# A transformer block's forward and backward pass: bulk transfers behind transposed rows, a later kv^T block, and gate-gradient chunks one block ahead

## The chip, the cores and the metric

The kernel runs on one core of a Trainium2 chip. The metric is the device time of one execution in microseconds (us), and less is better. The core has five engines that work side by side, each through its own instructions in order: TensorE (PE, with its weight loads shown as PEld), VectorE (DVE), ScalarE (ACT), GpSimd (POOL) and SyncE (SP), which in this kernel only issues transfers (DMAs). Engines wait for each other by semaphores.

## The reference

One transformer block with pre-layernorms, linear attention and a gated MLP, its output and its gradients. B = 1, S = 2048 rows, D = 640, H = 32 heads of 20, F = 1728, all in bf16. In short:

```python
def A(x, wqkv, wo):                       # linear attention
    q, k, v = split_heads(x @ wqkv)
    phi = lambda t: where(t > 0, t + 1, exp(t)) + 1e-6
    pq, pk = phi(q), phi(k)
    kv = einsum("bhsd,bhse->bhde", pk, v)
    z  = einsum("bhsd->bhd", pk)
    den = einsum("bhqd,bhd->bhq", pq, z)[..., None] + 1e-6
    return merge_heads(einsum("bhqd,bhde->bhqe", pq, kv) / den) @ wo

def B(x, w1, w3, w2):                     # gated MLP
    return (silu(x @ w1) * (x @ w3)) @ w2

h  = x + A(layernorm(x), wqkv, wo)
h2 = h + B(layernorm(h), w1, w3, w2)      # output 0
# outputs 1 to 6: gradients of sum(h2 * grad_out) for x, wqkv, wo, w1, w3, w2
```

## The kernel before

The rows are worked on in 16 tiles of 128 (t = 0 to 15) and in four chunks of 512 rows (c = 0 to 3). The order of the instructions on every engine is the order in which the program is written; only the memory pools and their semaphores are filled in by the framework. The stages around the change are these.

**Stage 1, the loop over t in range(ST).** For each tile, `p1_mm(t, D)` makes k from the transposed normalized rows `pqT`, and `phi` evicts it with two ACT activations (L294, L295) and two DVE operations that are held back (`held`) and run later (L298, L299). `v_steps[t]` lists what DVE does in step t: "S" is the statistics of a tile (`stat`), "N" its normalization on DVE (`p1_norm`), R one held-back piece. "A", "B" and "L" are normalizations after `phi`: "A" ahead of `q_tile`, "B" and "L" behind it. Even tiles above 8 are normalized on ACT (L165), the others on DVE (L160). For tiles from 8 on `p1_norm` also issues, on SP, the transposing DMA of that tile's rows into `pqT` (L250); the matmuls of `p1_mm(t)` wait for it. The big transfers go through the same queue: `trickle` says after which tile a piece of w1, w3 or wqkv is loaded, and `outs` after which tile the normalized rows (`xn_out`) and phi(k) (`group_out`) are stored. Each x load, `load_x(a, b)`, brings tiles a to b - 1.

**Stage 2, after that loop.** `m_part(m, tiles)` accumulates block m of the product of phi(k) and the normalized rows; `m_end` evicts it and transposes it into `mT`; `kvT_block(m, acc)` multiplies it with the v weights (L448) and writes its masked diagonal blocks to `bd` with one DVE multiply (L211). Between them `q_tile(t)` makes q of a tile, and `r_row(t)` makes the denominators on DVE (L373 to L380). The accumulators of `kvT_block` and `q_tile` alternate between the two buffers of the PSUM tag "big". Then `ps.release()` ends that PSUM pool and the pool "pap" takes the same banks. Its first steps are `q_late(10, f2_mT)`, where `f2_mT` (L717, tile `trm`, tag "at") transposes the last block of m between the two halves of q of tile 10.

**Stage 3, the MLP loop.** Block n = c * FT + fc, with FT = 14. `mlp(c, fc, ...)` first calls `mlp_ghh`, which makes a chunk of the gate gradient's input, `ghh` (five matmuls of 512 columns and an ACT eviction, L419), for a later block; `ghh` tiles hold two chunks and have four buffers. Then come gate and up (L394), ACT's four evictions, part of the second product of the chunk before (`o2_steps`), and side steps: `f2_at` (attention output of the next chunk's tiles, L654), `f2_hn` (their second layernorm, with a store of the rows) and `f2_ht` (the transposing DMA of these rows). `drain` runs one of seven DVE operations per pair of blocks (L829) at a time. `r_steps[c][fc]` lists further steps: `r_den` and `r_end` (denominators of tiles 8 to 15, using PSUM tag "at", which `f2_at` uses too) and loads.

The rest, the backward products, is not touched by the change.

## Time and profile before

| | us |
|---|---|
| three timed runs | 822.13, 822.12, 821.39 (median 822.12) |
| the profiled execution | 820.91 |
| its span in the profile | 819.1 |
| PE busy in the span | 814.1 |
| DVE busy | 452.4 |
| ACT busy | 323.6 |
| GpSimd busy | 130.9 |

Every value comes from one program on one core. The times are of runs without a profile, and the span is that of one execution with it, 1.8 us shorter than that execution's own time. TensorE's granted clock is full in all but the first moments. Instruction rows in the profile give the start in us from the span's start, the duration, the engine, the source line, the operation and the tile written <- tiles read.

### The profile page before, as it was taken

How to read it: one execution, taken by the hardware profiler on the slowest of the kernel's cores; microseconds unless marked ns; L12 is line 12 of the kernel's file. 1: busy time of each engine (PE TensorE's matmuls, PEld its weight loads, DVE VectorE, ACT ScalarE, POOL GpSimd, SP SyncE). 2: the span in 40 equal slices, each digit the busy share in tenths (PEclk: the TensorE clock that was granted, in tenths of full speed). 3: DMA queues.
4: the chain of work that ended last, by engine and by line, in shares of the span. 5: the costliest groups of instructions: out<-in, count | busy, mean ns of one | idle time of the engine just before them, and what ended most of it. 6: DMA issues, size and time to landing. Idle time of an engine off the chain costs nothing.

```text
span 819.1 us, 13944 instructions
## 1 busy us (share of the span) xinstructions
PE 814.1 (99%) x5420; PEld 512.8 (63%) x5420; DVE 452.4 (55%) x973; ACT 323.6 (40%) x603; POOL 130.9 (16%) x193
## 2 busy tenths in 40 slices
PE   9999999999999999999999999999999999999998
PEld 6677544555555555777777777777777777544444
DVE  7859987998898566300057777772781544200000
ACT  7856688665565666011122212222212334211111
POOL 2233333333222212100001111110220000000000
PEclk9999999999999999999999999999999999999999
DMA  9899699796485556999977877259974997967751
GB/s 264 219 290 239 166 244 327 225 245 173 127 211 156 169 170 167 222 261 226 257 176 180 211 197 200 58 107 187 287 195 93 181 194 159 239 164 186 160 141 36
DMA packets 323873, 157.88 MB, mean 193 GB/s; under 512 B 242784, under 2 KB 317056, under 8 KB 323808
## 3 DMA queue, kind: packets, MB, share of 16 engines
q1 hardware_dynamic: 281040, 116.18, 61.6%
q0 software_dynamic: 7328, 24.48, 8.7%
q10 hardware_dynamic: 35440, 16.34, 7.7%
q8 instruction: 42, 0.69, 0.4%
q14 instruction: 23, 0.19, 0.1%
HBM read 47.09 MB, written 51.13 MB: 120 GB/s over the span
## 4 chain that ended last, share of the span: by engine, by line
PE 96%; DVE 2%; ACT 1%; issue 0%; DMA 0%; POOL 0%; ACTq 0%; DVEq 0%
PE mm L394 20%; PE job L1346 20%; PE ghn L1142 14%; PE gxn L1515 8%; PE gw L1097 7%; PE o L910 4%; PE o L856 3%; PE gwo L1230 3%; PE big L267 3%; PE gr L1199 3%; PE dkv L1452 3%; PE macc L429 2%; PE at L654 2%; PE mm L267 1%; PE dkv L1380 1%; DVE st L147 1%
## 5 line engine op out<-in xcount | busy, mean ns | idle before, releaser
L1346 PE MATMUL job<-gb,hnN 128*128 128x496 bf16 (+3 forms) x576 | 116.8, 366 | 0.0
L1142 PEld LDWEIGHTS <-ggb 128*128 128x128 bf16 x864 | 84.5, 98 | 32.8
L1346 PEld LDWEIGHTS <-hnN 128*128 128x128 bf16 x576 | 55.8, 98 | 61.0
L394 PE MATMUL mm<-pqT,w 128*128 128x512 bf16 x405 | 93.8, 379 | 0.1
L394 PEld LDWEIGHTS <-w 128*128 128x128 bf16 x540 | 52.5, 98 | 63.4 <-issue 1.4
L1350 ACT CAST obs<-job 128x496 bf16<-128x496 f32 (+4 forms) x56 | 28.5, 510 | 123.7 <-PE job L1346 120.9
L1142 PE MATMUL ghn<-w13a,ggb 128*128 128x320 bf16 x448 | 63.5, 299 | 0.0
L1157 DVE SCALAR_TENSOR_TENSOR wb<-gs,hnb 128x640 f32<-128x640 bf16 x16 | 13.2, 825 | 88.7 <-ACT gs L1154 88.7
L1142 PE MATMUL ghn<-w13b,ggb 128*128 128x320 bf16 x416 | 61.4, 299 | 0.0
L394 PE MATMUL mm<-g2T,w2T 128*128 128x512 bf16 x240 | 59.6, 379 | 0.0
L1097 PE MATMUL gw<-g,hb 128*128 128x320 bf16 x416 | 56.8, 299 | 0.0
L1207 POOL TENSOR_TENSOR sz<-Zb,g_h 128x640 f32<-128x640 bf16 x16 | 20.2, 1261 | 197.7 <-DVE g_h L1208 197.7
L1097 PEld LDWEIGHTS <-hb 128*128 128x128 bf16 x416 | 40.6, 98 | 16.0 <-issue 0.3
L419 ACT CAST ghh<-mm 128x512 bf16<-128x512 f32 x48 | 28.3, 589 | 47.7 <-PE mm L394 40.1
L793 ACT ACTIVATE sig<-mm 128x512 bf16<-128x512 f32 x56 | 33.9, 605 | 26.4 <-PE mm L394 21.1
L1154 ACT ACTIVATE gs<-ghn 128x640 bf16<-128x640 f32 x16 | 11.3, 704 | 78.8 <-PE ghn L1142 73.9
L394 PEld LDWEIGHTS <-w2T 128*128 128x128 bf16 x260 | 25.4, 98 | 23.4
L267 PEld LDWEIGHTS <-pqT 128*128 128x128 bf16 x320 | 30.7, 98 | 13.7 <-ACT pqT L259 1.5
L267 PE MATMUL big<-wqkv,pqT 128*128 128x320 bf16 x250 | 38.6, 299 | 0.6 <-ACT pqT L259 0.3
L1346 PEld LDWEIGHTS <-g 128*128 128x128 bf16 x320 | 31.0, 98 | 11.5
L829 DVE TENSOR_TENSOR gate<-gate,sig 128x1024 bf16<-128x1024 bf16 x28 | 19.3, 689 | 33.2 <-ACT gate L804 30.5
L910 PE MATMUL o<-w,hhT 128*128 128x320 bf16 x224 | 35.0, 299 | 0.0
(219 smaller groups left out, 1369.9 us busy)
## 6 DMA issues: line engine op xcount, KB each, us to landing
hh_d<-hhT SPq DMA_DIRECT2D x24, 256.0 KB, 2.7
gg_d<-gate POOLq DMA_DIRECT2D x24, 256.0 KB, 4.3
gg_d<-ghh POOLq DMA_DIRECT2D x24, 256.0 KB, 3.4
ggb<-gg_d SPq DMA_DIRECT2D x6, 896.0 KB, 5.4
ggb<-gg_d ACTq DMA_DIRECT2D x6, 832.0 KB, 5.7
ggb<-gg_d SPq DMA_DIRECT2D x2, 1728.0 KB, 12.7
x_sb<-in_A_x_dram SPq DMA_DIRECT2D x5, 640.0 KB, 5.9
pk_d<-pk_all SPq DMA_DIRECT2D x4, 640.0 KB, 6.6
```

The source lines that it names most:

```text
L267: T.matmul(acc, lhsT=pqT[:, c, t * P:(t + 1) * P], rhs=wqkv[:, c, n0:n0 + HD], start=(c == 0), stop=(c == DT - 1))
L394: T.matmul(acc[:], lhsT=w[:, c, fc * P:(fc + 1) * P], rhs=rhs[:, c, :], start=(c == 0), stop=(c == DT - 1))
L419: A.copy(out=ghh[n // 2][:, n % 2, :], in_=acc[:])
L793: A.activation(sig[:, i, :], gp[:], AF.Sigmoid)
L856: T.matmul(accs[i, j][:, 0:HD], lhsT=hhT[c][:, fc, i * P:(i + 1) * P], rhs=w2[:, fc, j * HD:(j + 1) * HD], start=(first and fc == 0), stop ...
L910: T.matmul(o2["ps"][:, 0:HD], lhsT=hhT[c][:, fc, i * P:(i + 1) * P], rhs=w2[:, fc, j * HD:(j + 1) * HD], start=(fc == 0), stop=(fc == FT - 1))
L1097: T.matmul(acc[:, j, 0:HD], lhsT=hb[b][:, t, i * P:(i + 1) * P], rhs=g2[:, t, j * HD:(j + 1) * HD], start=(t == 0), stop=(t == ST - 1))
L1142: T.matmul(acc[:, j, 0:HD], lhsT=ggb[t // 2][:, k, lo:lo + P], rhs=rhs[:, j * HD:(j + 1) * HD], start=(k == 0), stop=(k == NG - 1))
L1199: T.matmul(gr[t][:, j, 0:HD], lhsT=ghT[t][:, c, :], rhs=wT2[:, c, j * HD:(j + 1) * HD], start=(c == 0), stop=(c == DT - 1))
L1346: T.matmul(acc[:, 0:n], lhsT=lhs[:, t, m * P:(m + 1) * P], rhs=rhs(t), start=(t == 0), stop=(t == ST - 1))
L1350: A.copy(out=ob, in_=acc[:, 0:n])
L1515: T.matmul(acc[:, j, 0:HD], lhsT=g, rhs=wqT[:, k, j * HD:(j + 1) * HD], start=(k == 0), stop=(k == 14))
```

## The change

It leaves every computation as it is and moves steps:

- The load of x tiles 8 to 11 becomes one of tiles 8 and 9, and tiles 10 to 15 are loaded together after two weight loads.
- The first w3 piece is loaded after tile 7 instead of 5 of the stage 1 loop, and the store of the first group of phi(k) follows tile 9 instead of 8.
- The normalization of tile 14 comes ahead of `q_tile(3)` instead of behind it.
- `kvT_block(1)` comes behind `r_row(4)`, `r_prod(6)`, `phi_rest()` and six tiles of `m_part(4)`.
- In the MLP loop, `f2_ht` of tiles 4 and up follows the normalization directly, ahead of the store of the rows.
- From block 14 on, `mlp_ghh` makes chunk n + 1 in block n instead of n + 2; block 14 makes none, since block 13 still made chunk 15.
- The last w2T load of the MLP loop comes ahead of the reload of q of tile 8.

```diff
-    load_x(8, 12)
+    load_x(8, 10)
     load_w2T(2 * P, 4 * P)
     load_wq(0, 2)
-    load_x(12, ST)
+    load_x(10, ST)
...
-    trickle = {4: w13[0], 5: w13[1], 9: lambda: load_wq(4, 6), 12: w13[2], 14: w13[3]}
+    trickle = {4: w13[0], 7: w13[1], 9: lambda: load_wq(4, 6), 12: w13[2], 14: w13[3]}
...
-               9: (("N", 13), R, ("S", 14), ("B", 12)), 10: (R, R, ("S", 15)), 11: (R, ("B", 14), ("L", 15))}
+               9: (("N", 13), R, ("S", 14), ("B", 12)), 10: (R, R, ("S", 15)), 11: (R, ("A", 14), ("L", 15))}
...
-    outs = {7: ((xn_out, 0, dma),), 8: ((group_out, 0),), 12: ((group_out, 1), (xn_out, 1, dma)), 13: ((group_out, 2),)}
+    outs = {7: ((xn_out, 0, dma),), 9: ((group_out, 0),), 12: ((group_out, 1), (xn_out, 1, dma)), 13: ((group_out, 2),)}
...
     q_tile(8)
-    kvT_block(1, big())
     r_row(4)
     r_prod(6)
     phi_rest()
     m_part(4, range(5, 11))
+    kvT_block(1, big())
     q_tile(9)
...
         ln2.norm(hn[t][:], x_sb[:, t, :], t)
-        if t < 2:
+        if t < 2 or t >= TPC:
             f2_ht(t)
...
-        if n >= FILL - AHEAD:
-            mlp_ghh(n + AHEAD)
+        if FILL - AHEAD <= n < FT or n > FT:
+            mlp_ghh(n + (AHEAD if n < FT else 1))
...
-            for k, pos, f in ((k0 + 2, 1, f2_at), (k0 + 3, 0, f2_hn), (k0 + 3, 1, f2_ht)):
+            for k, pos, f in ((k0 + 2, 1, f2_at), (k0 + 3, 0, f2_hn)):
...
-    r_steps = [{0: ((load_x, 6, 8),), 1: ((r4_out, 0, 2),), 2: ((r_load, 8),), 3: ((load_w2T, 10 * P, F),), 4: ((r_load, 9), (r4_out, 2, 4)),
+    r_steps = [{0: ((load_x, 6, 8),), 1: ((r4_out, 0, 2),), 2: ((load_w2T, 10 * P, F),), 3: ((r_load, 8),), 4: ((r_load, 9), (r4_out, 2, 4)),
```

More of the change, by code (lines that the diff above doesn't have):

```diff
@@ L967, in sides @@
                     f = f2_at0
-                if k0 == -2 and f in (f2_at0, f2_hn, f2_ht):
+                if k0 == -2 and f in (f2_at0, f2_hn):
                     k, pos = (k + 1, 0) if f is f2_at0 else (k + 1, pos)
@@ L999, in run_side @@
             if c + 1 < SC:
-                for f, i in sorted(sides[c][pos].get(fc, ()), key=lambda x: (x[0] is f2_ht, x[1])):
+                for f, i in sorted(sides[c][pos].get(fc, ()), key=lambda x: x[1]):
                     f((c + 1) * TPC + i)
```

## The prediction

> **What bounds the kernel now.** The page comes first: its parts 1 and 4, busy time by engine and the chain that ended last.

> ```profile
> PE 814.1 (99%) x5420; PEld 512.8 (63%) x5420; DVE 452.4 (55%) x973; ACT 323.6 (40%) x603; POOL 130.9 (16%) x193
> ...
> PE 96%; DVE 2%; ACT 1%; issue 0%; DMA 0%; POOL 0%; ACTq 0%; DVEq 0%
> ```

> TensorE (PE) is the bound, and the change takes no matmul away. So there is next to nothing to win: each wait that reaches PE is lost whole, and only PE's present holes could be gained. In the timeline those that lie near the edits are 0.28 us before 38.08, about 0.4 us at 96 to 98 and 0.28 us before 102.45, under 1 us together. The question is which new wait reaches PE. I read it from the order of instructions that the built program has, held against the timeline of each engine.

> **The kv^T block (the large term).** In the timeline, PE and then DVE where the block is moved (start, duration, engine, line, operation):

> ```profile
> 68.92 1.79 PE L429 MATMUL macc<-x_sb,pk_all 128*128 128x320 bf16 x12
> 70.55 1.52 PE L267 MATMUL big<-wqkv,pqT 128*128 128x320 bf16 x10
> 71.91 1.52 PE L429 MATMUL macc<-x_sb,pk_all 128*128 128x320 bf16 x10
> 73.27 0.84 PE L267 MATMUL mm<-wqkv,pqT 128*128 128x320 bf16 x5
> 73.94 0.51 PE L717 MATMUL trm<-ident,hx 128*128 128x128 bf16 x5
> ```

> ```profile
> 72.56 0.29 DVE L211 TENSOR_TENSOR bd<-bigx,mask 128x140 bf16<-128x140 f32 x1
> 72.77 0.86 DVE L373 TENSOR_REDUCE rden<-pr 128x16 f32<-128x320 f32 x2
> 73.67 0.48 DVE L376 TENSOR_SCALAR rden<-rden 128x32 f32<-128x32 f32 x1
> 74.18 0.35 DVE L377 RECIPROCAL rden<-rden 128x32 f32<-128x32 f32 x1
> 74.57 0.97 DVE L380 TENSOR_TENSOR pql<-pql,rden 128x640 bf16<-128x640 bf16 x1
> 75.46 0.31 DVE L298 TENSOR_SCALAR mq<-mq 128x640 bf16<-128x640 bf16 x1
> 75.88 0.49 DVE L299 TENSOR_TENSOR hx<-mq,rq 128x640 bf16<-128x640 bf16 x1
> ```

> On PE the move costs nothing: the block's five matmuls (68.61 to 68.92) change places with the twelve that follow, and q_tile(9) at 70.55 keeps its time. But the block brings its mask multiply (L211) along on DVE, and it now stands behind r_row(4) and phi_rest, which are the seven instructions from 72.77 on. They run without a hole, so the eight together end where they end now, at 75.88 + 0.49 = 76.37, with the mask last instead of first. Who waits for it? In both programs the first matmul of trm (f2_mT, L717) waits for exactly this mask multiply: the new PSUM pool puts trm on the bank that kvT_block(1) used. Now the mask ends at 72.56 + 0.29 = 72.85 and PE comes at 73.94, a cover of 1.09 us. Then PE waits until 76.37, and 0.05 us for the handover (at 38.08 it started 0.05 us after its releaser): 76.42 - 73.94 = 2.5 us. Behind trm on PE stands all that follows; DVE's later work is no later than now. The DVE chain starts from PE's own z_rows at 55.4 (POOL's pr waited 7.7 us for Zb), so PE delays before it move both sides alike. Bounds: 2.2 us if the run is a little quicker, 2.7 if a hole opens in it. What follows is ordered by PE, so I count nothing as given back.

> **SP's queue (w3 piece, x, group_out(0), the norm of tile 14).** SP in the timeline, then the answers on DMA for the issues around 38 and around 43 us (KB each, median us from issue to landing):

> ```profile
> 32.59 0.58 SPq L516 DMA_DIRECT2D xn_d<-x_sb  x1
> 33.22 0.51 SPq L520 DMA_DIRECT2D pk_d<-pk_all  x1
> 35.51 2.73 SPq L250 DMA_TRANSPOSE pqT<-x_sb  x2
> 38.29 0.57 SPq L183 DMA_DIRECT2D wqkv<-in_A_wqkv_dram  x1
> ```

> ```profile
> wqkv<-in_A_wqkv_dram SPq DMA_DIRECT2D x1, 800.0 KB, 4.7
> ```

> ```profile
> pqT<-x_sb SPq DMA_TRANSPOSE x2, 2.6
> ```

> After the change SP issues the transposed rows of tiles 8 to 11, xn_out(0), the w3 piece, tiles 13 and 12, group_out(0), the wqkv piece, tiles 14 and 15. Tile 9 gets 832 KB less in front: it took 4.6 us to land instead of the 2.6 of tile 8, yet its matmuls at 30.74 started without a hole, so this wins nothing that shows. Tiles 13 and 12 have w3 (832 KB) instead of group_out(0) (640 KB) ahead of them, but the queue is emptier at 31 us: about as now. Tile 14 is the loser. Now group_out(0), issued at 33.22, has landed 5.0 us later, before the wqkv piece goes out at 38.29; that lands at 43.0, and tile 14, issued at 41.79, lands 2.6 us later at 44.4, just ahead of its matmuls at 44.61. After, group_out(0) goes out at about 38.3 with the wqkv piece behind it. Back to back such a store adds 2.2 us (xn_d landed at 36.1, pk_d at 38.2). wqkv then lands at 43.0 + 2.2 = 45.2, or a microsecond sooner if tiles 12 and 13 free the queue early. A transposed tile behind a bulk transfer landed 0.8 us after it (tile 9 behind w3: 25.81 + 4.6 = 30.4 against 24.65 + 5.0 = 29.6) or 1.4 (tile 13 behind pk_d). So tile 14 lands between 44.6 and 46.5, against 44.4. Moving its norm ahead of q_tile(3)'s two activations makes it ready 1.2 us sooner, and that is of no use behind a full queue. Price 0.2 to 2.1 us; I take the middle, 1.2. Without queueing it is 0. Tile 15 follows tile 14 closely and finds PE late already.

> [...]

> **Gate-gradient chunks one block ahead.** From block 14 on ghh chunk n+1 is made instead of n+2. Block 14 makes none, block 53 makes one that it did not. A chunk is five 512-wide matmuls, 1.08 us (139.67 to 140.75). PE runs 1.08 us earlier through chunk c=1, and pays it back in c=3: zero, if nothing stops PE in between. One place does:

> ```profile
> 185.17 0.69 DVE L829 TENSOR_TENSOR gate<-gate,sig 128x1024 bf16<-128x1024 bf16 x1 [0.39 <-ACT gate L804]
> ```

> ```profile
> 189.85 0.88 DVE L373 TENSOR_REDUCE rden<-prp 128x16 f32<-128x320 f32 x2
> ...
> 190.50 1.25 PE L654 MATMUL at<-Wp,pqT 128*128 128x320 bf16 x8
> ```

> f2_at at 190.50 needs the bank that r_den(12)'s first reduction leaves, at 190.34 (half of its 0.88 us and the gap): cover 0.16 us. DVE is without a real hole from 142.2 to 185.17, so it gains only that 0.39 us. PE loses 1.08 - 0.16 - 0.39 + 0.05 = 0.6 us; bounds 0 and 1.08. The buffer that ACT waited for at 142.53 (0.36 us, a gg_d store) comes free in time, but PE did not wait there. GpSimd's memset of the tail chunk falls behind one more gg_d store; ACT's copies wait for PE alone.

> **Edits at nothing.** x in parts 8 to 10 and 10 to 16: the last part lands about where the last one did (13.94 + 8.6 = 22.5), and DVE first reads tile 10 at 26.93, cover 4 us; were it gone, DVE's unbroken run would pass the loss on. The norm of tile 14 holds up q_tile(3)'s eviction by 0.9 us; its bank is next used at 42.43, cover 1.5 us now. f2_ht ahead of the hn stores, and the last w2T piece ahead of r_load(8), put transposes earlier on SP; PE waited for none, and the stores that fall behind have no reader near.

> **Sum.** Against the profiled execution (820.91: span 819.1 and 1.8 around it): 2.5 + 1.2 + 0.6 = 4.3, so 825.2. The three timed runs lie 0.5 to 1.2 above that execution, median 822.12. Tiles 9, 12 and 14 land so close to their use that some of this may be waits of theirs, and tile 9's would go: I take back 0.3. 822.1 + 4.3 - 0.3 = 826.1, say 826.0.

> **Rivals.**
> - Tile 14 does not queue: 2.5 + 0.6 = 3.1, less 0.3: 824.9. For it: the queue is empty for moments around 43 us, and tile 14 is ready earlier. Against: every landing above came in issue order.
> - The hole cools PE's clock. In this trace PE runs at half rate at the start: 34 warm-up matmuls of 128 columns took 3.81 us, 0.11 each, against 0.056 for the transposes in the chain at 16 us, and the slow spell lasts from 1.1 to about 7 us. [...] It decides if the hole is long enough; no hole here shows what is. [...]
> - Not slower: DVE reaches the mask in time. The point is a mask that ends before 73.9, which needs the seven instructions to start 2.5 us earlier relative to PE than now; then trm costs nothing, and with tile 14 in time and the f2_at wait small the rest is -0.3 to +0.6: 822.0. Against: POOL's pr and DVE start from PE, and the seven have no hole to close.
> - Faster by more than 0.2%: that would need the hole absent and all 1.2 us by which the timed runs exceed the profile, and some of PE's other holes, recovered: 820.2.

> **How the numbers follow.** Forecast (all three terms) 0.58, tile 14 in time 0.27, cooled clock or a longer hole 0.07, no hole 0.05, faster 0.03. A measurement can tell about 0.2% (1.6 us) from no change, so slower means over 823.8: the first three cases, 0.92. The range goes from the second case with its terms at their low ends (2.2 + 0.3 - 0.9, taking back most of the 1.2: 823.7) to the forecast with tile 14 at 2.1 and the chunk term at 1.08 (827.8).

> **What would show it.** Right: trm's first matmul starts 0.05 us after a bd<-bigx mask that ends some 2.4 us after PE stood ready; tile 14's rows land after wqkv, with a PE hole ahead of its matmuls; a hole of about half a microsecond ahead of f2_at in c=1. Wrong: trm's matmul follows the q_late matmuls without a hole, or PE's matmuls show half rate behind it.

## The result, and the profile after

The changed kernel takes 827.22 us (median of five executions, 826.26 to 828.30) against 821.42 for the kernel before beside it: 1.0065 times the time, with an interval of 1.005 to 1.008. The forecast was 826.0 (823.7 to 827.8). The profiled execution took 826.82, span 825.0 against 819.1: 5.9 us more.

From the page, its parts 1 and 4, busy time by engine and the chain that ended last:

```profile
PE 812.5 (98%) x5392; PEld 512.3 (62%) x5420; DVE 452.9 (55%) x973; ACT 323.6 (39%) x603; POOL 130.9 (16%) x193
...
PE 87%; DVE 8%; DMA 2%; issue 1%; SPq 1%; ACT 1%; POOL 0%; DVEq 0%; ACTq 0%; POOLq 0%
```

DVE's busy time is nearly as before, and no matmul was taken away (28 of PE's records are missing from this trace, so its busy sum says little). But the chain runs through DVE, SP and transfers for longer than before: PE waits for them. To see where, I took the start of one and the same matmul in both traces and followed the difference along the program:

| stretch | PE's delay grows by, us | term in the prediction |
|---|---|---|
| start to tile 14's matmuls (47.16) | 2.56 | 1.2, less 0.3 taken back |
| trm | 2.42 | 2.5 |
| first MLP block (107.8) | 0.57 | 0 |
| gate-gradient chunk: earlier by 1.08, f2_at waits, 1.08 paid back in c=3 | 0.31 | 0.6 |
| sum, before rounding | 5.87 | 4.0 |

**trm.** The timeline of PE, then of DVE, at the moved block:

```profile
74.47 1.52 PE L429 MATMUL macc<-x_sb,pk_all 128*128 128x320 bf16 x10
75.83 0.84 PE L267 MATMUL mm<-wqkv,pqT 128*128 128x320 bf16 x5
79.00 0.44 PE L717 MATMUL trm<-ident,hx 128*128 128x128 bf16 x5 [2.33 <-DVE bd L211]
```

```profile
76.94 0.97 DVE L380 TENSOR_TENSOR pql<-pql,rden 128x640 bf16<-128x640 bf16 x1
77.83 0.31 DVE L298 TENSOR_SCALAR mq<-mq 128x640 bf16<-128x640 bf16 x1
78.24 0.49 DVE L299 TENSOR_TENSOR hx<-mq,rq 128x640 bf16<-128x640 bf16 x1
78.65 0.29 DVE L211 TENSOR_TENSOR bd<-bigx,mask 128x140 bf16<-128x140 f32 x1
```

The mask is now the last of DVE's run; it ends at 78.65 + 0.29 = 78.94, and trm starts 0.06 us later. Of this wait the profile counts 2.33 us as idle time of PE; from start to start, by the matmuls behind trm, it is 2.42 us. Before, the two lines of PE stood at 73.27 and 73.94 with nothing between them.

**Tile 14.** SP's queue in the timeline, then the answers on DMA (KB each, us from issue to landing) for the issues around 38.7 and 41.0, then PE:

```profile
38.04 0.58 SPq L520 DMA_DIRECT2D pk_d<-pk_all  x1
38.66 0.51 SPq L183 DMA_DIRECT2D wqkv<-in_A_wqkv_dram  x1
40.99 3.22 SPq L250 DMA_TRANSPOSE pqT<-x_sb  x2
```

```profile
wqkv<-in_A_wqkv_dram SPq DMA_DIRECT2D x1, 800.0 KB, 7.8
pk_d<-pk_all SPq DMA_DIRECT2D x1, 640.0 KB, 4.7
```

```profile
pqT<-x_sb SPq DMA_TRANSPOSE x1, 6.1
```

```profile
44.37 0.98 PE L429 MATMUL macc<-x_sb,pk_all 128*128 128x320 bf16 x6
47.16 1.12 PE L267 MATMUL big<-wqkv,pqT 128*128 128x320 bf16 x7 [1.82 <-DMA pqT<-x_sb]
```

group_out(0) lands at 42.8, the wqkv piece at 38.66 + 7.8 = 46.5, tile 14's rows at 47.1, where before the piece took 4.7 us and the rows 2.6. They were issued 0.8 us earlier than before and landed 2.8 us later.

### The profile page after: what moved, and what is told of

It reads as the page before. It is cut to its first block, busy times and chain, and to the rows that moved or that the text cites. A ratio compares the mean times of both kernels' runs of the same rounds, so it can differ in the third digit from the quotient of the medians.

```text
span 825.0 us, 13903 instructions
## 1 busy us (share of the span) xinstructions
PE 812.5 (98%) x5392; PEld 512.3 (62%) x5420; DVE 452.9 (55%) x973; ACT 323.6 (39%) x603; POOL 130.9 (16%) x193
## 4 chain that ended last, share of the span: by engine, by line
PE 87%; DVE 8%; DMA 2%; issue 1%; SPq 1%; ACT 1%; POOL 0%; DVEq 0%; ACTq 0%; POOLq 0%
PE job L1346 19%; PE mm L394 16%; PE ghn L1142 14%; PE gxn L1515 8%; PE gw L1097 7%; PE o L856 3%; PE gwo L1230 3%; PE big L267 3%; PE gr L1199 3%; PE dkv L1452 3%; PE o L910 2%; PE at L654 2%; PE macc L429 1%; DVE s L829 1%; PE mm L267 1%; DMA g2T<-in_grad_out_dram 1%
## 5 line engine op out<-in xcount | busy, mean ns | idle before, releaser
L267 PE MATMUL big<-wqkv,pqT 128*128 128x320 bf16 x250 | 38.4, 299 | 2.0 <-DMA pqT<-x_sb 1.8
L267 PEld LDWEIGHTS <-pqT 128*128 128x128 bf16 x320 | 30.5, 98 | 15.7 <-DMA pqT<-x_sb 2.1
L829 DVE TENSOR_TENSOR gate<-gate,sig 128x1024 bf16<-128x1024 bf16 x28 | 19.3, 689 | 35.4 <-ACT gate L804 32.7
```

Source lines behind the costliest of these rows:

```text
L267: T.matmul(acc, lhsT=pqT[:, c, t * P:(t + 1) * P], rhs=wqkv[:, c, n0:n0 + HD], start=(c == 0), stop=(c == DT - 1))
L829: V.tensor_tensor(out=out, in0=a, in1=b, op=alu)
```

## The experiments

Twelve kernels ran in three groups, each group on one chip beside the kernel before. Names with a_ start from the changed kernel, with b_ from the kernel before.

| run | median, us | before beside it | ratio (interval) |
|---|---|---|---|
| a_kv_back | 824.44 | 822.33 | 1.0022 (1.0009 to 1.0035) |
| a_trm_mm | 825.79 | 822.33 | 1.0040 (1.0027 to 1.0052) |
| a_w3_back | 826.33 | 822.33 | 1.0047 (1.0034 to 1.0060) |
| a_out_back | 828.54 | 822.33 | 1.0081 (1.0067 to 1.0095) |
| b_queue | 823.12 | 822.37 | 1.0011 (0.9999 to 1.0022) |
| b_x_split | 822.25 | 822.37 | 0.9996 (0.9988 to 1.0005) |
| b_ghh | 822.36 | 822.37 | 0.9997 (0.9987 to 1.0006) |
| b_free | 823.90 | 822.37 | 1.0024 (1.0013 to 1.0036) |
| a_again | 827.56 | 822.11 | 1.0060 (1.0044 to 1.0076) |
| a_fill | 827.22 | 822.11 | 1.0062 (1.0047 to 1.0077) |
| b_kv | 824.43 | 822.11 | 1.0035 (1.0020 to 1.0050) |
| b_q_out | 822.15 | 822.11 | 0.9998 (0.9989 to 1.0007) |

### The kv^T block

a_kv_back:

```diff
     q_tile(8)
+    kvT_block(1, big())
     r_row(4)
...
     m_part(4, range(5, 11))
-    kvT_block(1, big())
```

> The changed kernel with kvT_block(1) back ahead of r_row(4). Theory of the kv^T term: trm waits because the mask multiply stands behind seven DVE instructions; with the block back the mask ends about a microsecond before PE comes to trm, the 2.42 us hole ahead of trm (76.5 to 79.0 in the changed kernel's trace) is gone whole, nothing takes it back, and the time falls by 2.4: 827.2 to 824.8 (2.9 left of the 5.8 lost, with what stays of tile 14 and the rest). Rival: DVE is late there anyway, because tile 14's hole pushed it; then trm still waits 0.5 us or more and the time falls by less than 1.9.

Its PE at trm, in the timeline:

```profile
75.74 0.84 PE L267 MATMUL mm<-wqkv,pqT 128*128 128x320 bf16 x5
76.42 0.51 PE L717 MATMUL trm<-ident,hx 128*128 128x128 bf16 x5
```

The hole is gone whole, though tile 14's hole was still there (1.93 us of idle time at 47.07), so the rival falls. PE's delay against the kernel before is 3.52 us behind c=0 to 3, against 5.87: 2.35 less, as expected; the median came to 824.44.

a_trm_mm, which changes only the PSUM tile that trm writes:

```diff
-        tr = ps.tile([P, DT, P], BF16, name="trm", tag="at", bufs=2)
+        tr = ps.tile([P, DT, P], BF16, name="trm", tag="mm", bufs=4)
```

> The changed kernel with only trm's PSUM tile moved from tag at to the four-bank tag mm; the block stays late. Theory: the wait is one of a PSUM bank and not of data. Then trm follows q_late's first half without a hole, and the next user of the mask's bank, kv^T block 2 (15 matmuls later, 1.6 us), waits instead: the mask ends at 78.94 in the changed kernel's trace and PE would come at 80.64 - 2.42 = 78.2, so a hole of 0.7 to 0.8 us there, and 1.7 us less in all: 825.5. Rival: PE really needs the mask's result, or the whole DVE run, there; then the hole stays 2.4 us and the time 827.2.

```profile
76.47 0.51 PE L717 MATMUL trm<-ident,hx 128*128 128x128 bf16 x5
76.81 1.52 PE L267 MATMUL mm<-wqkv,pqT 128*128 128x320 bf16 x10
78.95 1.11 PE L448 MATMUL kv<-mT,wqkv 128*128 128x160 bf16 x15 [0.62 <-DVE bd L211]
```

The same work waits for nothing at trm and for the mask at block 2, where the bank went: 0.79 us from start to start against 0.7 to 0.8 expected. So the wait is for the bank, not for data. Up to the end of the MLP loop PE's delay is 4.23 us against 5.87, so 1.64 less, as expected. That the median of 825.79 lies near the expected 825.5 is partly chance: 825.5 was counted down from 827.22, an execution slowed by the clock (below), and the profiled execution lost another 0.75 us at 340 us, in a stretch that no edit touches.

b_kv, the move alone (`kvT_block(1, big())` put behind `m_part(4, range(5, 11))` in the kernel before):

> The kernel before with only kvT_block(1) moved behind m_part(4, 5 to 10). Theory: a hole of 2.4 to 2.5 us ahead of trm as in the changed kernel, given back nowhere: 2.4 us over the kernel before in executions whose clock stays at 1.0, and about 4 in those where the hole cools the clock (after such a hole the kernel with group_out(0) back ran at a granted clock of 0.53 for 3 us, which cost it 1.6 us more). Median 2.4 to 4 over the kernel before. Rival: some of it is given back behind trm (a hole of PE that closes); then less than 2.

```profile
76.45 0.44 PE L717 MATMUL trm<-ident,hx 128*128 128x128 bf16 x5 [2.32 <-DVE bd L211]
```

The hole was again there, 2.32 us of idle time ahead of trm, nothing was given back behind it in the trace (PE ends 2.46 us later), and the median rose by 2.3, just under the low end of what was expected. The twelve executions fall into two sets: seven at a mean clock of 1.0 with a median of 823.87, five at 0.998 with 827.17. I come back to these. The seven lie only 1.8 us above the 822.11 of the kernel before, not 2.4; where the rest went no profile shows. The kernel before has waits of its own in some executions (next section).

### SP's queue

a_w3_back and a_out_back each undo one of the two moves:

```diff
-    trickle = {4: w13[0], 7: w13[1], 9: lambda: load_wq(4, 6), 12: w13[2], 14: w13[3]}
+    trickle = {4: w13[0], 5: w13[1], 9: lambda: load_wq(4, 6), 12: w13[2], 14: w13[3]}
```

> The changed kernel with the w3 piece back at tile 5 (issued about 24.7 us instead of 33.0); group_out(0) stays behind tile 9. Theory Q (bytes): tile 14's rows are late because 832 KB more stand ahead of them in the queue in the stretch from 32 us, whichever transfer goes last; without w3 there they land by about 44.9 (PE needs them about 45.2), the hole of 2.0 us ahead of their matmuls falls to 0.4 or less, and the time is about 1.7 lower: 825.5. Theory O (order): it is group_out(0) that was put right ahead of the wqkv piece and of tile 14; then 1 us or more of the hole stays and the time is 826.2 or more.

```diff
-    outs = {7: ((xn_out, 0, dma),), 9: ((group_out, 0),), 12: ((group_out, 1), (xn_out, 1, dma)), 13: ((group_out, 2),)}
+    outs = {7: ((xn_out, 0, dma),), 8: ((group_out, 0),), 12: ((group_out, 1), (xn_out, 1, dma)), 13: ((group_out, 2),)}
```

> The changed kernel with group_out(0) back behind tile 8; the w3 piece stays behind tile 7. Theory Q (bytes): the same bytes stand ahead of tile 14, now also ahead of tiles 12 and 13; a hole of 1 to 2 us opens at tile 12 or 13 (37 to 41 us) in place of most of tile 14's, and the time stays within 0.7 of 827.2. Theory O (order): the hole at tile 14 closes and none opens; 825.4.

PE's waits for transposed rows in the timeline of a_w3_back, then of a_out_back:

```profile
32.39 2.89 PE L267 MATMUL big<-wqkv,pqT 128*128 128x320 bf16 x20 [1.31 <-DMA pqT<-x_sb]
46.80 1.40 PE L267 MATMUL big<-wqkv,pqT 128*128 128x320 bf16 x9 [0.64 <-DMA pqT<-x_sb]
```

```profile
42.88 1.53 PE L267 MATMUL big<-wqkv,pqT 128*128 128x320 bf16 x10 [2.80 <-DMA pqT<-x_sb]
```

Neither theory holds whole. With w3 back, tile 14's rows still landed at 46.75, behind group_out(0) and the wqkv piece: theory Q expected 44.9 and is wrong there. Its hole is small only because PE came later, held up by tile 9 behind the w3 piece. With group_out(0) back, theory O is wrong: tile 14's hole closed, but a larger one opened at tile 12, whose rows waited behind w3 and group_out(0). PE had lost as much by tile 14's matmuls as in the changed kernel (2.63 us against 2.56), so the 1.3 by which the time rose is not the queue's: all five executions ran at a mean clock of 0.998 or less (below). What fits both: either transfer, moved later, stands ahead of the next tile whose rows are wanted, and that tile pays. It needs no full queue: from 32 to 47 us the mean DMA share is 1.04 in the changed kernel and in a_out_back, but 0.80 in a_w3_back, where group_out(0) right ahead of the wqkv piece made tile 14 late all the same.

b_queue, both moves alone in the kernel before:

> The kernel before with only the w3 piece at tile 7 and group_out(0) at tile 9; x in its old parts, everything else old. Theory Q (bytes ahead of tile 14): these two edits alone make the hole of 1.5 to 2.5 us ahead of tile 14's matmuls (a part of it at tile 12 if the w3 piece lands late), and 0.3 us at 38 closes: 1.2 to 2.0 over the kernel before. Rival: the x split is what fills the queue; then the holes at tiles 12 to 14 stay under 0.7 us in all and the time is within 0.5 of the kernel before.

```profile
40.63 1.53 PE L267 MATMUL big<-wqkv,pqT 128*128 128x320 bf16 x10 [0.23 <-DMA pqT<-x_sb]
47.02 1.26 PE L267 MATMUL big<-wqkv,pqT 128*128 128x320 bf16 x8 [1.85 <-DMA pqT<-x_sb]
```

Its profiled execution lost 0.23 us of idle time at tile 12 and 1.85 at tile 14, some 2.4 us from start to start, with x in its old parts: the two moves do it alone. But in twelve executions the median rose by only 0.75, and the interval runs from nothing to 1.8 us. A likely reason for a part of this is in the run of b_q_out below, whose first 60 us of SP are those of the kernel before:

```profile
29.84 0.98 PE L429 MATMUL macc<-x_sb,pk_all 128*128 128x320 bf16 x6
32.13 1.13 PE L267 MATMUL big<-wqkv,pqT 128*128 128x320 bf16 x7 [1.31 <-DMA pqT<-x_sb]
```

In that execution the old order cost 1.31 us at tile 9, where the profiled execution of the kernel before had 0.145 us to spare. Of the six traces with the w3 piece ahead of tile 9, two have this hole (a_w3_back and b_q_out); the seven with the w3 piece behind tile 9 have none there. So the moves trade a wait that the old order has in some executions for one that the new order had in every profiled one (PE's delay at tile 14's matmuls is 1.24 to 2.63 us in seven traces).

b_x_split, the x loads alone (`load_x(8, 10)` and `load_x(10, ST)`):

> The kernel before with only x loaded as 8 to 10 and 10 to 16. My prediction put this at nothing. Theory N (nothing): tile 9's rows land near 30.5 as in the kernel before, no hole near 30.8, time within 0.5 of the kernel before. Theory X: with the longer last part of x the w1 piece behind it lands about a microsecond later (26.0 to 26.5 in the four runs with the split, against 24.7), the w3 piece and tile 9 follow, tile 9 lands near 32.3 as in the run with w3 back, PE has a hole of 1.0 to 1.6 us near 30.8, and the time is 0.8 to 1.5 over the kernel before.

Tile 9's rows landed at 31.0 and PE did not wait for them, and the time is that of the kernel before: theory N, the prediction's "nothing", holds on the clock. The trace says less, since PE was itself 0.37 us late from about 10 us on; without that, rows at 31.0 would have met matmuls at 30.74. The late w1 piece (26.2 here) is not the split's doing: it landed at 26.1 in b_queue and 26.5 in b_q_out, which lack the split, and at 24.6 in a_again, which has it.

b_free, meant to be faster:

```diff
-    trickle = {4: w13[0], 5: w13[1], 9: lambda: load_wq(4, 6), 12: w13[2], 14: w13[3]}
+    trickle = {4: w13[0], 9: lambda: load_wq(4, 6), 12: w13[2], 14: w13[3]}
...
-    outs = {7: ((xn_out, 0, dma),), 8: ((group_out, 0),), 12: ((group_out, 1), (xn_out, 1, dma)), 13: ((group_out, 2),)}
+    outs = {7: ((xn_out, 0, dma),), 12: ((group_out, 1), (xn_out, 1, dma)), 13: ((group_out, 0), (group_out, 2))}
...
-        (f2_wT, 4), (phi_rest,), (q_late, 14), (r_T, 4), (r_head, 5), (r_prod, 7),
+        (f2_wT, 4), (phi_rest,), (q_late, 14), (r_T, 4), (r_head, 5), (r_prod, 7), (w13[1],),
```

> A version meant to be faster than both: the kernel before with the w3 piece out of the stretch of tiles 8 to 15 altogether (issued behind the transposes of Wp, near 90 us, where the queue is empty; its first reader is at 98.9) and group_out(0) issued with group_out(2), behind tile 15. Theory Q: 1.47 MB less stand ahead of tiles 9 to 14, so their rows land with a microsecond or more to spare, no hole of PE between 20 and 60 us in any execution: 0.3 to 1.0 us below the kernel before. Rival: the bytes return as a wait behind tile 15 (the rows of mT, landing 68.1 with 0.4 us of cover in the kernel before) or at 98 us; then a hole there and the same time or more.

```profile
69.32 0.48 PE L448 MATMUL bigx<-mT,wqkv 128*128 128x140 bf16 x5 [0.54 <-DMA mT<-hx]
```

No rows were late between 20 and 60 us, and the time still rose by 1.5: the rival. group_out(0) now stands ahead of the rows of mT, which had 0.4 us to spare. From start to start PE lost 0.72 us there and 0.67 at the first MLP block, at a wait that the section on the prediction explains.

### The gate-gradient chunks

b_ghh has only this edit:

> The kernel before with only the gate-gradient chunks one block ahead. Theory: PE runs 1.08 us earlier through chunk c=1, waits 0.3 us at f2_at in block 10 of c=1 (0.32 to 0.35 us in the five traces that have the edit) and pays the rest back at the end of c=3; 0.3 over the kernel before. The cover there is larger than the 0.55 us that I took. Rival: the 0.3 us were a result of the later start (other edits); then no hole there and the time is the same.

```profile
189.75 1.52 PE L654 MATMUL at<-Wp,pqT 128*128 128x320 bf16 x10 [0.15 <-DVE rden L373]
```

The hole is there without the other edits (0.31 us from start to start), so the rival falls; in the measured time it can't be told from no change.

### The clock behind the hole

Among the first five executions of the changed kernel, two had a mean granted clock of 1.0 (826.26, 826.82) and three 0.998 (827.22 to 828.30). a_again is the changed kernel once more:

> The changed kernel itself again, beside the next three. In its first five executions the core's mean granted clock was 1.0 twice (826.3 and 826.8) and 0.998 three times (827.2 to 828.3). Theory C: PE's hole ahead of trm (2.4 us), or tile 14's (2.0), cools the clock in some executions; again some 4 to 6 of 10 executions lie 1 to 2 us above the others with a mean clock of 0.998, median 827. Rival: that was that chip; then all lie at 826.5.

This time the profiled execution was one of the slower ones. Stretches of a_again, then of the first execution (busy PE and its matmuls, granted clock, DMA share, GB/s):

```profile
core 0: us, PE busy (x), PEclk, DMA share, GB/s
76.00:79.00 3.00, 0.81 (x9) 1.00 0.91 175
79.00:82.00 3.00, 3.00 (x20) 0.50 0.88 313
82.00:86.00 4.00, 4.00 (x42) 0.95 0.00 0
```

```profile
76.00:79.00 3.00, 0.68 (x5) 1.00 1.05 230
79.00:82.00 3.00, 3.00 (x34) 1.00 0.82 241
```

The hole is the same, 2.33 us of idle time ahead of trm in both. Behind it PE ran at a granted clock of 0.50 for about 3.4 us in a_again (20 matmuls from 79 to 82 us where the other did 34), and its delay grew there by 4.08 us instead of 2.42. a_out_back shows the same fall (0.53 in this stretch) and the same 4.09.

The traces also show where the two differ. Their clock records give the slow spell as 79.03 to 82.44 us in a_again and 79.16 to 82.58 in a_out_back, 3.41 us long, and full clock as beginning at 3.93 and 4.07, so 75.09 us or 22 times 3.413 us earlier. Counted off in steps of 3.413 us from there, the hole lies whole inside the step that ends at the fall in both traces. In the first execution, where full clock began at 5.53, a step ends at 77.21 inside the hole, and neither step holds more than 1.8 us of it. In none of the fourteen traces does the clock fall behind a step with 1.93 us of idle time or less. In all fourteen the last fall, behind the end of PE's work, lies whole steps from the onset too (238 to 241; it is 812.37 us or 238 steps in the kernel before and 819.20 us or 240 in the first execution of the changed one). That the place of the hole in these steps decides on the fall is my reading of these traces; no run moved it there on purpose, so it is not shown.

All eleven executions of the changed kernel: four at 1.0, median 826.4; seven at 0.998, median 827.8.

a_fill keeps the wait and takes away the idleness:

```diff
     def f2_mT():
+        warm_up(40, ps.tile([P, 512], F32, name="idle", tag="mm", bufs=4))
```

> The changed kernel with 40 matmuls of 128 columns on constant data put on PE just ahead of trm, into a free tile of tag mm (their result is not used): some 2.2 us of work where PE waits 2.4 us for the mask. Theory C (the hole cools the clock in some executions): the wait is not shortened, so the best executions stay at 826 to 826.5, but the executions at a mean clock of 0.998 go (all but those that tile 14's 2.0 us hole makes): at least 0.7 us off the median, 826.3. Rival: the late executions come from elsewhere (transfers); then as many lie above 827.5 as in the changed kernel, and the median stays at 827.2 or rises.

All six executions had a mean clock of 1.0, where seven of eleven had fallen. That half of theory C is borne out. The other half is not: the best execution is 826.34 as expected, but the median stayed at 827.22.

```profile
75.18 2.40 PE L467 MATMUL idle<-ones 128*128 128x128 bf16 x40
77.66 0.44 PE L718 MATMUL trm<-ident,hx 128*128 128x128 bf16 x5
```

In the profiled one the filler costs nothing at trm (2.48 us from the fill's start to trm's; PE's delay grows there by 2.41, against 2.42 without), and it took 826.34. It had lost only 1.24 us by tile 14's matmuls, and 0.75 at 340 us as in a_trm_mm. What delayed the others, at full clock, no profile here shows, and it stays open. Counted over all runs, a mean clock of 0.998 or less came in 19 of 33 executions of kernels with the trm hole, in none of 45 of those where trm's wait was short or filled and no profiled hole passed 1.8 us (a_trm_mm, a_fill, b_ghh, b_x_split, b_q_out), in 2 of 19 with tile 14's hole as the longest (a_kv_back, b_queue), and in 3 of 12 of b_free, whose profile has no hole over about a microsecond; why there, is open. Of the 69 executions of the kernel before that ran beside these kernels, none fell below 0.999.

### One more try to be faster

b_q_out issues GpSimd's store of the late q tiles some 10 us earlier:

```diff
-        (f2_wT, 4), (phi_rest,), (q_late, 14), (r_T, 4), (r_head, 5), (r_prod, 7),
+        (f2_wT, 4), (phi_rest,), (q_out, 10, 14), (q_late, 14), (r_T, 4), (r_head, 5), (r_prod, 7),
...
-        (f2_half, 3, 1), (f2_m_out,), (q_out, 10, 14),
+        (f2_half, 3, 1), (f2_m_out,),
```

> A version meant to beat both: the kernel before with only GpSimd's store of the late q tiles (q_out, pq_d from pkx, 640 KB) issued about 10 us earlier, behind the phi of tiles 10 to 13. In every trace the first sigmoid of the MLP starts 0.23 us after that store has landed, and PE's hole near 102 to 107 us (0.28 to 1.04 us) follows from it. Theory: the hole closes, nothing else moves: 0.3 to 0.8 us below the kernel before. Rival: the sigmoid, or PE's fourth mm bank, then waits for another thing (DVE's run at 101, hn's rows) and the time is the same within 0.2.

The hole at 102 us closed, a hole of 0.35 us from start to start opened at 90.9 where PE waits for Wp's rows, and the time is the same. No version here beats the kernel before.

## Why the prediction was right, and where its sum was short

The direction, the three places and their mechanisms were right; the sum was 4.0 us and the profiled execution shows 5.87. That the median lies inside the range is partly luck: it holds 0.6 us missed at the first MLP block and, in the execution that is the median, a slow clock that the range did not count, while the sum started from 822.1 and the kernel before beside it took 821.42.

- **kv^T block, 2.5 us.** Right in place, mechanism and size (2.42). a_kv_back takes it away, a_trm_mm moves it to the next user of the bank, b_kv makes it alone (on the clock, in its executions at full clock, 1.8).
- **Tile 14, 1.2 us.** The mechanism (its rows behind group_out(0) and the wqkv piece) was right, and the first rival, that the rows do not queue, is refuted. The term was mis-sized: PE had lost 2.56 us by tile 14's matmuls. The working has a slip: wqkv at 44.2 to 45.2 and rows 0.8 to 1.4 us behind it give 45.0 to 46.6, not 44.6 to 46.5, and so a price of 0.6 to 2.2. But the rows landed later still, at 47.1. The step that failed is the landing of the wqkv piece, put at 45.2. The w3 piece that stands ahead of tiles 13 and 12 in place of group_out(0) made tile 12's rows 0.55 us later, not "about as now"; group_out(0) added 2.2 as predicted; and the piece itself took 3.7 us behind group_out(0), where it had taken 3.0 behind tile 12's rows. Together 3.4 us later, 46.5. The rows came 0.7 us behind it, less than either of the two distances I had. This execution had also waited 0.75 us for g2T at 15.3, a transfer ahead of every edit; a_kv_back and a_trm_mm lacked that wait and still lost 2.5 by tile 14, since PE stood idle there until the rows landed. The size is one execution's: with the same edits the wqkv piece landed at 45.7 in a_again and 45.1 in a_fill, and PE had lost 1.76 and 1.24 us there. So 45.2 was near the early end of what these edits give, and what sets the spread is open.
- **Gate-gradient chunks, 0.6 us.** Right in place; 0.31, because DVE made up 0.65 of the 1.08 us and not 0.39.
- **Edits at nothing.** True in the measured time of the x split, which was run alone. The others were not; PE shows no hole where I costed them, so for these it is read from the trace and not shown by a run.
- **What was missed.** The first sigmoid of the MLP waits for GpSimd's store of pkx, 0.23 us behind its landing in both traces. Before, PE was covered by its four mm banks but for 0.28 us. Now the store took 5.0 us instead of 4.5. The store in the kernel before, then in the changed kernel, and the sigmoid:

```profile
pq_d<-pkx POOLq DMA_DIRECT2D x1, 640.0 KB, 4.5
```

```profile
pq_d<-pkx POOLq DMA_DIRECT2D x1, 640.0 KB, 5.0
```

```profile
106.40 0.60 ACT L793 ACTIVATE sig<-mm 128x512 bf16<-128x512 f32 x1 [2.59 <-PE mm L394]
```

  The releaser that the line names, PE, had been done since 104; the store landed at 106.17. b_q_out, which issues the store earlier, closes the hole. In b_free and b_queue the store took 5.1 and 5.0 us and PE's delay grew by 0.67 there too, so it is no effect of one edit; what makes the store slower is not shown.
- **What I took back, 0.3.** It stood for waits at tile 9. Tile 9's margin was worth more: it fails in some executions of the old order, by some 1.5 us from start to start in b_q_out. That is a likely part of why two moves that cost 2.4 us in a profile cost about 0.75 in medians. The hole of 0.28 us at 38 us closed too, which the sum did not have. The range's upper end of 827.8 leaves the 0.3 out; with it, it is 827.5, which still holds the median.
- **The cooled clock**, a rival with a chance of 0.07: it is no rival but a second price on the same hole, paid in 7 of 11 executions. No trace of the kernel before shows what such a fall costs behind a hole; a_again shows 1.66 us (4.08 less 2.42). Nor does the length of the hole alone decide: it was 2.33 us in a_again, behind which the clock fell, and in the first execution, where it stayed at 1.00. The chance was far off. At full clock the kernel takes 826.4, close to the 826.0 forecast; the median of 827.22 is one of the cooled executions. Part of that closeness is the starting point: from 821.42, the kernel before beside the first five, it is a rise of 5.0 and not of 4.0.

## What to carry to other kernels

Before a producer is moved, list what its consumers on the other engines stand behind in their own order: five matmuls were free to move on PE, but the multiply that empties their bank went behind seven instructions of DVE, and a later tile of another name wanted that bank (trm, 2.42 us later for it). The bulk transfers moved out of one tile's way here were put into the next tile's way (2.56 us lost by tile 14's matmuls), so follow the queue to its end before counting a gain. And where margins are a tenth of a microsecond (tile 9's was 0.145 us), one trace shows one throw: measure several executions, and look at the granted clock of each.

## What the runs showed of the hardware that was not expected

In all fourteen traces each of the 329 transfers that SP issues landed in the order of issue, so a transposed tile of 160 KB waited out the 800 KB ahead of it: in the changed kernel the wqkv piece landed at 46.5 and tile 14's rows at 47.1. (The transfers take eight semaphores in turn. Between transfers of different semaphores the order is measured; within one semaphore the profile assumes it.)
